# Weight conversion moved to VectorE alone, beside the first attention, staged through DRAM and read back by every batch, with longer key and query rows

## The chip, the cores and the metric

The kernel runs on one core of a Trainium2 chip. Its time is the device time of one execution in microseconds (us). Before the change it was 932.59 us as the median of 3 runs (931.72 to 932.88).

## The reference, cut to what matters

```python
# attention: batch 4, 8 heads, 768 tokens, head size 64; block-sparse
#   local scores (|i-j| < 16) and scores against 24 block maxima of k,
#   one softmax over both, times v and the block means of v
x = attention(q, k, v)                       # (4, 768, 512)
# Fourier mix and a channel MLP
u  = x + real(fft(fft(x, axis=1), axis=2))
un = (u - mean(u)) / sqrt(var(u) + 1e-6)
out = u + maximum(un @ w_ch1, 0) @ w_ch2     # w_ch1 512 x 2048, w_ch2 2048 x 512, both float64
```

The inputs q, k and v are float32. The two weight matrices come as float64 and have to be turned into float32 on the core, from pairs of 32-bit integers.

## The kernel before

Each batch goes through attention (four steps of two heads), a Fourier part, a layer norm, and a channel part. The channel part computes both products by the seven-product scheme for 2x2 blocks, so it needs sums of weight blocks: seven 128x256 pieces a block. There are 16 weight blocks: eight of the first matrix and eight of the second. The channel part is cut in four stages: `h` with half of the first matrix, `o` with half of the second, and again. TensorE does batch b's channel part while the attention of batch b+1 is interleaved. A scheduler orders the built instructions by itself.

Batch 0 has to make the weights. A block is two conversions (four VectorE steps, two ScalarE steps, one GpSimd multiplication each) and four GpSimd sums. They go straight into the buffer that batch 0 reads, and one write-back puts the block into DRAM for batches 1 to 3.

In the profile lines PE is TensorE, DVE VectorE, ACT ScalarE, POOL GpSimd and SPq SyncE's queue of transfers. `raw` are the integers as loaded, `cvt` the steps of a conversion, `w` a weight block in its buffer, `m` a staged block, `dw` its copy in DRAM, `s` sums of h for the second product, `kn` the keys as loaded, `km` their block maxima. `y` are Fourier products, `hx`, `hy`, `hz` products with the first matrix, `ox`, `oy`, `oz` with the second. The "fold" is VectorE's sums that open the Fourier part.

```python
def convert(name, dst, src, shape):                      # half a block: 128 x 512
    raw = bpool.tile([P, n, 2], I32, tag="raw", bufs=2)
    nc.sync.dma_start(out=raw..., in_=src)
    # 2 VectorE bit operations, 2 ScalarE activations, 2 VectorE operations (lines 687 to 693)
    gtt(dst, vb, va, ALU.mult)                           # GpSimd

def make_w1(j):
    w = bpool.tile([P, 7, 2, P], FP, tag="w1", bufs=3)   # the buffer batch 0 multiplies from
    for hh in range(2):
        convert(f"1_{j}_{hh}", w[:, 2 * hh:2 * hh + 2]..., src, (NDT, P))
    _left_sums(gtt, lambda i: w[:, i])                   # 4 sums on GpSimd
    nc.sync.dma_start(out=dw1[j], in_=w)                 # one write-back
    wt[1, 0, j] = w
# make_w2 likewise, tag "w2", 4 buffers

def load(b, g):                                          # rows of 64 floats = 256 bytes
    for dst, src in ((kn, k), (qn, q)):
        for e in range(2):
            nc.sync.dma_start(out=dst[:, :, e, :], in_=src[b, 2 * g + e].rearrange("(t p) d -> p t d", p=P))
...
    drive((gen_attention(0), 1))
    get_tables(0)                    # tables of the Fourier products
    drive((gen_weights(0, 3), 1))    # three blocks
    for b in range(B):
        gens = [(gen_post(b), 4)]    # Fourier part and channel part, four steps a round
        if b == 0:
            gens.append((gen_weights(3, None), 1))   # one block a round
        if b + 1 < B:
            gens.append((gen_attention(b + 1), 1))
        drive(*gens)
```

Of the kernel before, what the change touches and what calls it, by code (L numbers as in the profile page):

```python
# [469 lines left out]
def _main_program(ctx, tc, q, k, v, moe_w_ch1, moe_w_ch2, out):  # L470
# [63 lines left out]
    def load(b, g):  # L534
        qn, kn = (apool.tile([P, NST, 2, D], FP, tag="nat", bufs=4, name=f"{n}n_{b}_{g}") for n in "qk")
        for dst, src in ((kn, k), (qn, q)):
            for e in range(2):
                nc.sync.dma_start(out=dst[:, :, e, :], in_=src[b, 2 * g + e].rearrange("(t p) d -> p t d", p=P))
        nat[b, g] = qn, kn
# [42 lines left out]
    def prepare(b, g):  # L582
# [3 lines left out]
        for src, dst in ((kn, kt[:, W:W + S]), (qn, qt)):  # L586
            for h in range(2):
                ps = abank([P, HT, P], f"qk_{b}_{g}_{h}")
                for i in range(HT):
                    nc.tensor.transpose(ps[:, i, :], src[:, HT * h + i].rearrange("p e d -> p (e d)"), ident)  # L590
                nc.scalar.copy(out=dst[:, S2 * h:S2 * (h + 1)], in_=ps.rearrange("p i c -> p (i c)"))
# [33 lines left out]
    def values(b, g, p, pm, x):  # L625
# [19 lines left out]
        for r in range(2):  # L645
            rc = rec[:, b * NP + g, r]
            nc.vector.reciprocal(out=rc, in_=av[r][:, :, D])
            for h in range(2):
                ts, c = slice(HT * h, HT * (h + 1)), P * g + D * (r ^ h)
                tt(x[:, ts, c:c + D], av[r][:, ts, 0:D], rc[:, ts, None].to_broadcast([P, HT, D]), ALU.mult)  # L650
# [25 lines left out]
    wt = {}  # L676

    def convert(name, dst, src, shape):
# [17 lines left out]
        gtt(dst, vb, va, ALU.mult)  # L696

    def make_w1(j):

        w = bpool.tile([P, 7, 2, P], FP, tag="w1", bufs=3, name=f"w1_0_{j}")  # L700
        for hh in range(2):
            c = DF // 2 * hh + P * j
            src = moe_w_ch1.bitcast(I32)[:, 2 * c:2 * (c + P)].rearrange("(d p) n -> p d n", p=P)
            convert(f"1_{j}_{hh}", w[:, 2 * hh:2 * hh + 2].rearrange("p a d n -> p (a d) n"), src, (NDT, P))
        _left_sums(gtt, lambda i: w[:, i])
        nc.sync.dma_start(out=dw1[j], in_=w)
        wt[1, 0, j] = w

    def make_w2(j):

        w = bpool.tile([P, 7, HD], FP, tag="w2", bufs=NC, name=f"w2_0_{j}")
        for hh in range(2):
            r = P * (NJ * hh + j)
            convert(f"2_{j}_{hh}", w[:, 2 * hh:2 * hh + 2], moe_w_ch2.bitcast(I32)[r:r + P, :].rearrange(
                "p (a n) -> p a n", a=2), (2, HD))
        _right_sums(gtt, lambda i: w[:, i])
        nc.sync.dma_start(out=dw2[j], in_=w)
        wt[2, 0, j] = w

    def get_w1(b, j):  # L720
        w = bpool.tile([P, 7, 2, P], FP, tag="w1", bufs=3, name=f"w1_{b}_{j}")
        nc.sync.dma_start(out=w, in_=dw1[j])
        wt[1, b, j] = w

    def get_w2(b, j):
        w = bpool.tile([P, 7, HD], FP, tag="w2", bufs=NC, name=f"w2_{b}_{j}")
        nc.sync.dma_start(out=w, in_=dw2[j])
        wt[2, b, j] = w

    def gen_weights(first, last):  # L730

        steps = [(f, j) for c in range(0, NJ, NC) for f in (make_w1, make_w2) for j in range(c, c + NC)]
        for f, j in steps[first:last]:
            f(j)
            yield
# [4 lines left out]
    def get_tables(b):  # L740
        tag, bufs = ("w1", 3) if b else ("w2", NC)
        fs = []
        for par in range(2):
            t = bpool.tile([P, 2, HT, F2 + 1], FP, tag=tag, bufs=bufs, name=f"fs_{b}_{par}")
            nc.sync.dma_start(out=t, in_=dr["fs"].ap()[par])
            fs.append(t)
        fd = bpool.tile([P, 6, HD], FP, tag=tag, bufs=bufs, name=f"fd_{b}")
# [4 lines left out]
    def gen_fourier(b):  # L752
# [28 lines left out]
        for par in range(2):  # L781
            for g in range(4):
# [10 lines left out]
                nc.vector.tensor_copy(out=tr[:, g, par:S2:2], in_=ps[:, F2:0:-1])  # L793
# [4 lines left out]
        for half in range(2):  # L798
# [24 lines left out]
            for _ in range(4):  # L823
                tt(z, y, y, ALU.mult)
                tt(z, z, var, ALU.mult)
                nc.vector.tensor_scalar(out=z, in0=z, scalar1=-0.5, scalar2=1.5, op0=ALU.mult, op1=ADD)
                tt(y, y, z, ALU.mult)
            norms.append((stat, y))

        for t in range(NST):  # L830
            half, i = divmod(t, HT)
            stat, y = norms[half]
            nc.vector.tensor_scalar(out=un[:, t, :], in0=x[:, t, :], scalar1=stat[:, i, 0:1], scalar2=y[:, i:i + 1],
                                    op0=SUB, op1=ALU.mult)
# [3 lines left out]
            (nc.scalar.copy if t % 2 else nc.vector.tensor_copy)(  # L838
# [5 lines left out]
    def gen_channel(b):  # L844
        x, u = x_of[b], wt["u", b]
        for c in range(NJ // NC):
            js = range(NC * c, NC * (c + 1))
            if b:
                for j in js:
                    get_w2(b, j)  # L850
            h = bpool.tile([P, NC, 2, S], FP, tag="h", name=f"h_{b}_{c}")
            for j in js:
                if b:
                    for n in range(j if j == 0 else j + 2, min(j + 3, NJ)):
                        get_w1(b, n)
# [10 lines left out]
                def relu(t):  # L866
                    nc.vector.tensor_scalar(out=t, in0=t, scalar1=0.0, scalar2=None, op0=ALU.max)  # L867
# [5 lines left out]
                relu(c11)  # L873
# [4 lines left out]
                nc.scalar.copy(out=c22, in_=Z)  # L878
                yield
                product(X, S3, T3, False, False)  # L880
                tt(c22, X, c22, ADD)
                relu(c22)
                product(Z, S4, B22, False, True)
                tt(c12, Z, c12, ADD)
                relu(c12)
                yield
                product(X, A22, T4, False, True)
                nc.scalar.activation(out=c21, in_=X, func=AF.Relu)
                yield
# [72 lines left out]
    drive((gen_attention(0), 1))  # L962
# [62 lines left out]
```

## Time and profile before

| | before |
|---|---|
| span of the profiled run | 929.2 us |
| first Fourier product / first channel product of batch 0 | 80.4 / 137.2 us |
| end of batch 0's channel part | 350.6 us |
| the four channel stages | 53.5, 62.1, 52.4, 45.4 us |
| batches 1 to 3 | 578.6 us |

The prediction below shows the view by stretches that these come from. The first line is from the page's list of engines: busy us, share of the span, instructions.

```profile
PE 829.2 (89%) x6386; PEld 618.3 (67%) x6386; DVE 530.3 (57%) x1158; ACT 168.8 (18%) x349; POOL 147.4 (16%) x142
```

The second is what the one queue from which SyncE issues nearly all transfers waited for in the first 330 us: line, releaser, us in total, times, longest.

```profile
SPq L706 <- POOL w L529: 60.6, 8, 17.9
SPq L717 <- POOL w L529: 48.2, 8, 10.7
```

Lines 706 and 717 are the write-backs. They stand 109 us waiting for GpSimd's sums.

### The profile page before, as it was taken

How to read it: one execution, taken by the hardware profiler on the slowest of the kernel's cores; microseconds unless marked ns; L12 is line 12 of the kernel's file. 1: busy time of each engine (PE TensorE's matmuls, PEld its weight loads, DVE VectorE, ACT ScalarE, POOL GpSimd, SP SyncE). 2: the span in 40 equal slices, each digit the busy share in tenths (PEclk: the TensorE clock that was granted, in tenths of full speed). 3: DMA queues.
4: the chain of work that ended last, by engine and by line, in shares of the span. 5: the costliest groups of instructions: out<-in, count | busy, mean ns of one | idle time of the engine just before them, and what ended most of it. 6: DMA issues, size and time to landing. Idle time of an engine off the chain costs nothing.

```text
span 929.2 us, 15289 instructions
## 1 busy us (share of the span) xinstructions
PE 829.2 (89%) x6386; PEld 618.3 (67%) x6386; DVE 530.3 (57%) x1158; ACT 168.8 (18%) x349; POOL 147.4 (16%) x142
## 2 busy tenths in 40 slices
PE   4778748687886799999999999999999997999997
PEld 3656634466753588657875888668857875587586
DVE  1366986799368964935423937635327556352252
ACT  2222312432023102221112012220021011200200
POOL 2230625567056700020000000000000000000000
PEclk9777859989898999999999999999999998999999
DMA  9995791777926508826162147321051161213101
GB/s 187 178 189 164 236 178 62 219 228 218 163 76 244 199 35 287 151 97 147 35 206 78 57 150 232 86 80 41 27 197 60 46 261 54 105 41 153 45 24 48
DMA packets 127917, 122.76 MB, mean 132 GB/s; under 512 B 102912, under 2 KB 111328, under 8 KB 127840
## 3 DMA queue, kind: packets, MB, share of 16 engines
q1 hardware_dynamic: 127296, 121.14, 46.9%
q8 instruction: 52, 0.85, 0.4%
q10 hardware_dynamic: 544, 0.56, 0.2%
q14 instruction: 25, 0.20, 0.1%
HBM read 100.71 MB, written 20.97 MB: 131 GB/s over the span
## 4 chain that ended last, share of the span: by engine, by line
PE 68%; DVE 20%; DMA 4%; POOL 3%; issue 3%; SPq 2%; ACT 1%; DVEq 0%; ACTq 0%; POOLq 0%
PE ox L906 17%; PE hx L863 15%; PE oz L906 8%; PE hz L863 7%; PE oy L906 4%; PE hy L863 4%; PE y L786 3%; DMA raw<-in_moe_w_ch_dram 2%; DVE cvt L688 2%; POOL w L529 2%; DVE cvt L693 2%; PE sc L606 2%; DVE cvt L691 2%; DVE x L526 2%; DVE cvt L687 2%
## 5 line engine op out<-in xcount | busy, mean ns | idle before, releaser
L863 PE MATMUL hx<-u,w 128*128 128x384 f32 x512 | 189.2, 500 | 15.5 <-ACT h L876 6.0
L863 PEld LDWEIGHTS hx<-u,w 128*128 128x128 f32 x512 | 97.9, 195 | 85.8 <-ACT h L876 8.9
L906 PE MATMUL ox<-w,h 128*128 128x256 f32 x384 | 93.9, 393 | 8.4 <-DVE x L526 7.9
L863 PE MATMUL hz<-u,w 128*128 128x384 f32 x256 | 96.6, 498 | 4.7 <-ACT h L878 4.7
L906 PE MATMUL ox<-w,s 128*128 128x256 f32 x384 | 92.8, 384 | 4.0 <-DVE x L526 3.5
L906 PE MATMUL oz<-w,s 128*128 128x256 f32 x384 | 93.0, 384 | 2.6 <-DVE s L526 2.6
L906 PEld LDWEIGHTS ox<-w,h 128*128 128x128 f32 x384 | 75.4, 197 | 22.8 <-DVE x L526 9.1
L906 PEld LDWEIGHTS ox<-w,s 128*128 128x128 f32 x384 | 72.0, 191 | 16.3 <-DVE x L526 5.6
L526 DVE TENSOR_TENSOR x<-ox,x 128x256 f32<-128x256 f32 x96 | 40.4, 422 | 74.2 <-PE ox L906 74.2
L906 PEld LDWEIGHTS oz<-w,s 128*128 128x128 f32 x384 | 73.3, 192 | 13.1 <-DVE s L526 2.9
L863 PEld LDWEIGHTS hz<-u,w 128*128 128x128 f32 x256 | 49.8, 195 | 40.3 <-POOL vb L529 5.3
L529 POOL TENSOR_TENSOR w<-cvt 128x512 f32<-128x512 f32 x32 | 43.6, 1364 | 133.2 <-DVE cvt L693 72.5
L529 POOL TENSOR_TENSOR w<-w 128x256 f32<-128x256 f32 x64 | 56.2, 893 | 3.1
L526 DVE TENSOR_TENSOR h<-hy,h 128x384 f32<-128x384 f32 x32 | 17.8, 555 | 67.5 <-PE hy L863 67.5
L526 DVE TENSOR_TENSOR h<-hx,h 128x384 f32<-128x384 f32 x32 | 17.8, 555 | 56.1 <-PE hx L863 56.0
L863 PE MATMUL hy<-u,w 128*128 128x384 f32 x128 | 46.5, 486 | 0.0
L906 PE MATMUL oy<-w,h 128*128 128x256 f32 x192 | 46.0, 380 | 0.3 <-POOL w L529 0.3
L606 PEld LDWEIGHTS sc<-qt,kt 64*64 64x64 f32 x1536 | 33.7, 157 | 12.7 <-issue 8.6
L606 PE MATMUL sc<-qt,kt 64*64 64x32 f32 x1536 | 36.7, 239 | 6.0 <-issue 3.7
L906 PEld LDWEIGHTS oy<-w,h 128*128 128x128 f32 x192 | 36.5, 191 | 5.8 <-POOL w L529 0.7
L867 DVE TENSOR_SCALAR h<-h 128x384 f32<-128x384 f32 x96 | 38.7, 404 | 2.9
L526 DVE TENSOR_TENSOR s<-h 128x512 f32<-128x512 f32 x48 | 39.2, 816 | 0.2
(92 smaller groups left out, 1043.3 us busy)
## 6 DMA issues: line engine op xcount, KB each, us to landing
w<-dw SPq DMA_DIRECT2D x48, 896.0 KB, 5.6
raw<-in_moe_w_ch_dram SPq DMA_DIRECT2D x32, 512.0 KB, 5.1
dw<-w SPq DMA_DIRECT2D x16, 896.0 KB, 4.3
vw<-in_v_dram SPq DMA_DIRECT2D x62, 192.0 KB, 5.7
kn<-in_k_dram SPq DMA_DIRECT2D x32, 192.0 KB, 5.3
qn<-in_q_dram SPq DMA_DIRECT2D x32, 192.0 KB, 5.2
vb<-in_v_dram SPq DMA_DIRECT2D x16, 384.0 KB, 6.3
out_dram<-x SPq DMA_DIRECT2D x24, 256.0 KB, 2.0
```

Source lines behind the costliest of these rows:

```text
L526: nc.vector.tensor_tensor(out=out, in0=in0, in1=in1, op=op)
L529: nc.gpsimd.tensor_tensor(out=out, in0=in0, in1=in1, op=op)
L606: nc.tensor.matmul(ps[h][r:r + 64, i, :], kt[rows, o:o + 64], qt[rows, o:o + BLOCK], start=True, stop=True)
L687: nc.vector.tensor_scalar(out=ex, in0=high, scalar1=0x7FF00000, scalar2=None, op0=ALU.bitwise_and)
L688: nc.vector.tensor_scalar(out=man, in0=high, scalar1=0x000FFFFF, scalar2=None, op0=ALU.bitwise_and)
L691: nc.vector.scalar_tensor_tensor(out=ex, in0=high, scalar=-(1 << 31), in1=ex, op0=ALU.bitwise_and, op1=ALU.bitwise_or)
L693: nc.vector.scalar_tensor_tensor(out=tmp[:, 1, :], in0=low, scalar=2.0 ** -52, in1=tmp[:, 1, :], op0=ALU.mult, op1=ALU.add)
L786: nc.tensor.matmul(y, fgs[par][:, st, P * g:P * (g + 1)], fs[par][:, g % 2, st, :], start=(st == 0), stop=(st == HT - 1))
L863: nc.tensor.matmul(ps, w[:, a, kk, :], u[:, r, kk, :], start=start and kk == 0, stop=stop and kk == 1, skip_group_check=True)
L867: nc.vector.tensor_scalar(out=t, in0=t, scalar1=0.0, scalar2=None, op0=ALU.max)
L906: nc.tensor.matmul(ps, left[a][:, n, :], wt[2, b, j][:, r, :], start=start and n == 0, stop=stop and n == NC - 1, skip_group_check=True)
```

## The change

Its intent: take GpSimd off VectorE's shared ports by converting on VectorE alone; begin the conversion where VectorE is idle, beside the first attention; free the making of weights from the buffers that hold them, by staging each block in small buffers into DRAM and reading it back in batch 0 too; and load keys and queries in rows of 1536 bytes instead of 256. A few small operations move to ScalarE or become fewer.

```diff
-            nc.sync.dma_start(out=dst[:, :, e, :], in_=src[b, 2 * g + e].rearrange("(t p) d -> p t d", p=P))
+            nc.sync.dma_start(out=dst, in_=src[b, 2 * g:2 * g + 2].rearrange("e (p t) d -> p e (t d)", p=P))
 ... prepare(): 8 ScalarE copies of 64 x 384 instead of 4 of 128 x 384 a group
-        gtt(dst, vb, va, ALU.mult)
-    def make_w1(j): ...
-    def make_w2(j): ...
+        tt(dst, vb, va, ALU.mult)
+    def gen_weights():
+        for c, f, j in [...]:
+            t = [bpool.tile([P, 2, HD], FP, tag="s", bufs=5, ...) for i in range(2)]
+            for hh in range(2):
+                convert(..., t[hh]...)
+                if hh == 0:
+                    yield
+            t += [... two more "s" buffers]
+            (_left_sums if f == 1 else _right_sums)(tt, lambda i: t[i // 2][:, i % 2])
+            for i, n in enumerate((2, 2, 2, 1)):
+                nc.sync.dma_start(out=to[:, 2 * i:2 * i + n], in_=t[i])     # four write-backs
+            yield
 ... batch 0 calls get_w1 and get_w2 (read-back) as batches 1 to 3 do; its tables use the "w1" buffers
 ... Newton: 3 x 3 + 1 small instructions instead of 4 x 4; half of the scalings on ScalarE;
 ... h clamps of batch 0 and mirrored Fourier copies on ScalarE; two divisions by the row sums in one
-    drive((gen_attention(0), 1))
+    weights = gen_weights()
+    drive((gen_attention(0), 1), ((next(weights) for _ in range(12)), 1))   # six blocks
     get_tables(0)
-    drive((gen_weights(0, 3), 1))
...
-            gens.append((gen_weights(3, None), 1))
+            gens.append((weights, 2))                                        # two half blocks a round
```

## The prediction

> **What bounds the kernel now.** I read first the view that cuts the span at the first Fourier product of each batch (80.4, 350.6, 549 and 746 us) and, inside batch 0, at the first product with each half of the weights: us, then busy us (and instructions) of the engines, granted TensorE clock, DMA share, GB/s.
>
> ```profile
> core 0: us, PE busy (x) PEld busy (x) DVE busy (x) ACT busy (x) POOL busy (x), PEclk, DMA share, GB/s
> 0.00:60.00 60.00, 39.74 (x975) 32.45 (x976) 16.77 (x57) 15.39 (x33) 13.48 (x18) 0.86 1.04 184
> 60.00:80.40 20.40, 12.91 (x272) 9.33 (x271) 16.36 (x33) 4.15 (x9) 4.38 (x4) 0.56 1.08 251
> 80.40:137.20 56.80, 40.37 (x362) 33.99 (x359) 47.63 (x116) 17.35 (x34) 23.67 (x23) 0.71 0.72 176
> 137.20:190.70 53.50, 43.27 (x233) 25.47 (x232) 39.97 (x62) 19.16 (x36) 26.11 (x27) 0.93 0.50 149
> 190.70:252.80 62.10, 52.00 (x400) 41.56 (x399) 50.09 (x82) 13.73 (x24) 29.75 (x27) 0.89 0.80 198
> 252.80:305.20 52.40, 40.94 (x113) 22.85 (x112) 37.77 (x51) 15.92 (x29) 29.88 (x29) 0.90 0.48 153
> 305.20:350.60 45.40, 39.72 (x195) 33.06 (x194) 35.80 (x61) 1.73 (x3) 14.28 (x10) 0.96 0.36 121
> 350.60:549.00 198.40, 194.67 (x1571) 145.82 (x1570) 104.72 (x253) 31.55 (x71) 5.86 (x6) 1.00 0.45 127
> 549.00:746.00 197.00, 195.14 (x1595) 146.21 (x1594) 102.56 (x257) 30.02 (x68) 0.00 (x0) 1.00 0.33 106
> 746.00:929.00 183.00, 170.43 (x686) 127.56 (x684) 78.62 (x191) 19.77 (x43) 0.00 (x0) 0.97 0.24 92
> ```
>
> There are two kernels in this one. From 350.6 us on TensorE is busy 560 of 578 us at a clock near 1: only 18 us are open there. Batches 1 and 2 do one batch's channel work plus the next one's attention in 197 to 198 us. Before 350.6 us the same kind of work (one more attention, some 25 us) takes 350 us, so about 125 us are stall or half clock. A change to the preparation of weights can only be worth something there.
>
> Within it, two limits. Up to 80 us the DMA engines are full:
>
> ```profile
> DMA packets 42640, 16.14 MB, mean 202 GB/s; under 512 B 40291, under 2 KB 41539, under 8 KB 42627
> q1 hardware_dynamic: 42083, 15.39, 102.2%
> ```
>
> Nine tenths of the packets of these 80 us are short ones, the 256-byte rows of q, k and v. Averaging the packet records of the trace, a 256-byte packet took 26 ns of an engine there, a 1024-byte one 56 ns (later), a 2048-byte one 90 ns, a 4096-byte one 245 ns.
>
> From 80 to 350 us it is VectorE and GpSimd together. One line each for two VectorE steps of the conversion and for GpSimd's multiplications (minimum/median/maximum ns):
>
> ```profile
> L688 DVE TENSOR_SCALAR cvt<-raw x32: 413/946/1502, 86.2 to 312.2; 128x512 int32<-128x512 int32 x32
> L693 DVE SCALAR_TENSOR_TENSOR cvt<-raw,cvt x32: 677/679/2836, 87.8 to 313.7; 128x512 f32<-128x512 uint32 x32
> L529 POOL TENSOR_TENSOR w<-cvt x32: 1260/1296/1698, 88.5 to 314.5; 128x512 f32<-128x512 f32 x32
> ```
>
> The same instruction on the same shape takes 0.41 us or 1.5 us: VectorE is being held up, and in order of time the long ones coincide with a GpSimd instruction. The waits of TensorE in this stage end on VectorE (the bracket is idle time and releaser):
>
> ```profile
> 74.64 1.67 PE L643 MATMUL av<-vs,psum 64*128 64x130 f32 x12 [3.96 <-DVE vs L526]
> 234.77 5.44 PE L906 MATMUL ox<-w,h 128*128 128x256 f32 x12 [3.82 <-DVE x L526]
> 325.71 3.50 PE L906 MATMUL ox<-w,h 128*128 128x256 f32 x8 [3.78 <-DVE x L526]
> ```
>
> After such a wait twelve products take 5.44 us where twelve later ones take 2.6: the stall is paid again in clock.
>
> **What the Trainium skill says.** "SBUF — State Buffer", section "Who interferes with whom": VectorE instructions in a 2-port mode, or with two SBUF inputs, share a port pair with GpSimd, and one side blocks fully. The trace agrees (0.41 against 1.5 us above). "DMA: Bandwidth & Descriptors", section "Specifications", asks for at least 512 bytes per transfer for line rate; the trace agrees in direction: 256 B in 26 ns is 9.8 GB/s per engine, 4096 B in 245 ns is 16.7. "TensorE: Matmul & The Clock Gate", section "What's actually happening": an idle TensorE falls to half clock; the 5.44 us above and the 0.56 in the second row agree.
>
> **The change, part by part.**
> 1. *GpSimd leaves the conversion.* Removed: 32 multiplications and 64 sums on GpSimd (43.6 + 56.2 us by the groups of costs). Added on VectorE: 32 of 128x512, 0.68 us each as the undisturbed sums of that shape in batches 2 and 3 (21.8), and 64 of 128x256 at 0.42 us (26.9, the duration of the undisturbed x sums of that size). Gained: the four VectorE steps cost 110 us now; at their minima (0.41 + 0.41 + 0.67 + 0.68) they cost 69.5. Net +8 us. The `h` clamps of batch 0 go to ScalarE (24 x 0.54 = -13 us), the mirrored Fourier copies too (-3), and other VectorE work in the stage loses its contention (`s` sums 0.89 to 1.2 us against 0.68, folds 1.2 against 0.95: about -12). So VectorE's 244 us before 350 us become some 225 although it does everything alone. This is the gain, but spread, not on one wait.
> 2. *Six weights are issued beside the first attention.* By the order of the built instructions four of 16 weight blocks stand before the first fold on VectorE. One costs 2 x 2.85 + 4 x 0.42 = 7.4 us, in starts some 6.5; four are 26 to 30 us, on an engine busy 16.8 of the first 60 us. It fits, if the raw bytes come.
> 3. *Longer rows.* A group's q and k are 3072 packets of 256 B now (5.0 us of 16 engines), then 512 of 1536 B (73 ns each, interpolated: 2.3 us). For the five groups loaded before the fold that saves 13 us. But the four blocks ask for eight raw loads (8 x 512 packets x 56 ns / 16 = 14 us) and write-backs (2.6 us each, 8 to 10 us). A full DMA stage gets 10 us fuller, and the first fold, at 59.7 us now, comes at about 74.
> 4. *Order on the queue and on VectorE.* In the new order the tables for the Fourier products are issued behind the write-back of the first second-matrix block, and a whole such block (6.5 us) stands on VectorE between the fold and the value sums that release TensorE. Fold 11 us, block 6.5, sums and the score products: first Fourier product at 98 instead of 80.4.
> 5. *The Fourier part of batch 0*: the order puts six more blocks (40 us of VectorE) between its steps; I take 52 us against 56.8. Channel work starts at 150 against 137, but with 10 blocks done where before there were four (8 of the 32 steps of line 688 lie before 137 us).
> 6. *The four channel stages*: 53.5 + 62.1 + 52.4 + 45.4 = 213 us now. TensorE's own work at full clock is 36 us each plus attention pieces (8 + 12 in the first two). I estimate 50 + 59 (two blocks stand before the first `s` sums, a stall of about 9) + 38 + 38 = 185. Batch 0 ends at 335 instead of 350.6: -15 us.
> 7. *Read-back in batch 0*: 16 more loads of 896 KB, 14.7 MB; landing takes 5.6 us and the DMA share there is 0.4 to 0.8. Hidden.
> 8. *Batches 1 to 3.* Newton's steps for the square root go from 4 x 4 to 3 x 3 small instructions plus one; half of the scalings go to ScalarE. In batch 3 this chain runs from 767.3 to 774.5 us with TensorE half idle: about -4. Batches 1 and 2 have 2 to 4 us of idle each: -1.5 each. Doubled ScalarE copies for q and k (8 of half height instead of 4 per group, 2 us more) have room: ScalarE is busy 32 of 198 us.
> Sum: -15 - 7 = -22, 932.6 to about 910.
>
> **Rivals.**
> *VectorE becomes the bound of batch 0 from the start.* It now is in the path of attention, conversion and Fourier, in order. For it: the raw loads stand behind buffer waits on one queue, so VectorE can idle on a load while an attention step stands behind it. Against it: its total falls. If the Fourier products start only at 110 us, the time is 922 to 930.
> *The first attention does not slow.* If loads hide as they did, the fold starts at 63 us and everything shifts by 11: 898. Together with channel stages at 43 us each once the contention is gone, 886.
> *The transfers take over.* The write-backs share five small buffers with the `s` sums; a write lands in 4.3 us but 6 to 7 in the full stage. If each block waits for the one before, blocks come every 12 us and the stage gives nothing: 932.
>
> **Range and chances.** The end is the sum of two uncertain terms: start of the Fourier products (98, by 10 either way) and stalls after it (by 10 either way), added in squares 14 us; later batches add 3. I put 909, nudged one down as my walk took loads at their slow landing, with 888 to 928 as the range. 2% lies at 914: faster 0.6, same 0.37, slower 0.03.
>
> **What would show it.** Right: VectorE's conversion steps all near 0.41 and 0.68 us; first Fourier product between 90 and 106 us; ten blocks converted before the first channel product; third and fourth channel stage under 40 us each; the next batch's Fourier products at 325 to 345; batches 1 to 3 together at 570 to 574 us. Wrong if the first Fourier product stays near 80 us, if TensorE waits for `w` loads in the channel stages, or if batches 1 and 2 lengthen by waits on the doubled ScalarE copies.

## The result, and the profile after

The changed kernel gives the right result and takes 941.0 us (940.05 to 942.08, 4 runs) against 932.15 us (928.89 to 932.88, 4 runs) of the kernel before on the same chip. The ratio is 1.010, with a 95% interval of 1.0075 to 1.013. A ratio is the mean time of one kernel's fast runs over that of the other's of the same rounds, so it is not quite the ratio of the medians quoted. The kernel is 1% slower; I had said 909 and a range up to 928.

The stretches of batch 0 after, with the columns of the first fence of the prediction. I cut at the first fold (83.7 us), the first Fourier product, the first product of each channel stage, and the next batch's first Fourier product.

```profile
0.00:83.70 83.70, 55.95 (x1020) 43.59 (x1020) 46.73 (x106) 37.71 (x71) 16.11 (x20) 0.68 0.87 218
83.70:114.80 31.10, 12.60 (x230) 9.46 (x226) 25.65 (x53) 10.61 (x20) 2.10 (x2) 0.55 0.72 208
114.80:166.40 51.60, 39.28 (x358) 31.67 (x358) 43.71 (x108) 22.53 (x48) 5.37 (x5) 0.79 0.76 248
166.40:214.70 48.30, 43.69 (x337) 25.99 (x335) 33.90 (x72) 24.63 (x49) 0.00 (x0) 0.96 0.81 271
214.70:292.10 77.40, 56.88 (x486) 46.74 (x485) 47.23 (x94) 18.86 (x35) 10.49 (x9) 0.80 0.78 211
292.10:328.20 36.10, 36.10 (x113) 21.28 (x112) 7.12 (x13) 13.45 (x27) 5.41 (x6) 1.00 0.54 191
328.20:364.50 36.30, 36.30 (x170) 31.78 (x169) 25.81 (x54) 0.53 (x2) 0.00 (x0) 1.00 0.16 53
```

Read the first column down. The first Fourier product comes at 114.8 us instead of 80.4. The Fourier part itself is shorter (51.6 against 56.8), and so are the first, third and fourth channel stage (48.3, 36.1, 36.3 against 53.5, 52.4, 45.4). The second is longer: 77.4 against 62.1. Batch 0 ends 13.9 us later, and batches 1 to 3 are 4.9 us shorter (573.7 against 578.6). The gain is there where it was foreseen, and more than its size is lost in two places. Up to the first Fourier product TensorE has the same 1246 products as before; of the 34.4 us that they take longer, 18.5 are idle time, and 15.9 are products that take longer at a lower granted clock (busy 68.6 us at 0.65, before 52.7 us at 0.78).

One caution for all tables by stage: the attention of batch 1 is interleaved with batch 0, and the scheduler orders it anew in each kernel. The four channel stages hold 1106 products here and 941 before, of which the channel part itself has 560 in each. So some of the longer second stage, and of the shorter batches 1 to 3, is attention done earlier: in batches 1 to 3 TensorE is busy 556.4 us against 560.2. Only the whole time compares kernels cleanly.

What TensorE waited for in the first 115 us; in the first 80 us of the kernel before the wait for k was 7.1 us, and the tables were not waited for.

```profile
PE qk L591 <- DMA kn<-in_k_dram: 27.1, 4, 7.9
PE y L785 <- DMA fs<-c_fs: 3.9, 1, 3.9
```

The DMA engines are busy 0.87 and 0.72 in these rows, less than the 1.04 and 1.08 of before, so their mean load does not explain a late k. It was issued late. Here is SyncE's queue (start us, duration us, what is issued), and its longest wait in the first 330 us (us in total, times, longest), to set beside the two lines of before:

```profile
37.00 2.26 SPq L721 DMA_DIRECT2D dw<-m  x3
39.35 1.99 SPq L578 DMA_DIRECT2D vw<-in_v_dram  x3
41.40 2.32 SPq L686 DMA_DIRECT2D raw<-in_moe_w_ch_dram  x2
43.76 0.69 SPq L538 DMA_DIRECT2D kn<-in_k_dram  x1
```

```profile
SPq L721 <- DVE m L526: 102.9, 34, 15.5
```

The write-backs (line 721) wait for VectorE's sums; the next raw load and the next k follow them. TensorE's two large waits in the second channel stage are of the same look, one for a read-back and one for the next batch's k:

```profile
229.14 1.22 PE L911 MATMUL ox<-w,h 128*128 128x256 f32 x2 [10.35 <-DMA w<-dw]
237.33 1.51 PE L591 MATMUL qk<-ident,kn 128*128 128x128 f32 x6 [6.12 <-DMA kn<-in_k_dram]
```

This made a tidy first theory, called head of line below: one queue, a write-back at its head that waits, urgent loads behind. The experiments leave little of it.

VectorE's steps did become short, as foreseen. These are groups of batch 0: busy us and mean ns of one.

```profile
L694 DVE SCALAR_TENSOR_TENSOR cvt<-raw,cvt 128x512 int32<-128x512 int32 x32 | 22.0, 689 | 6.5 <-ACT cvt L692 6.4
L691 DVE TENSOR_SCALAR cvt<-raw 128x512 int32<-128x512 int32 x32 | 13.6, 425 | 0.0
```

### The profile page after: what moved, and what is told of

It reads as the page before. It is cut to its first block, busy times and chain, and to the rows that moved or that the text cites. A ratio compares the mean times of both kernels' runs of the same rounds, so it can differ in the third digit from the quotient of the medians.

```text
span 938.2 us, 15352 instructions
## 1 busy us (share of the span) xinstructions
PE 837.2 (89%) x6386; PEld 625.4 (67%) x6386; DVE 498.1 (53%) x1106; ACT 233.1 (25%) x481; POOL 46.8 (5%) x46
## 5 line engine op out<-in xcount | busy, mean ns | idle before, releaser
L865 PE MATMUL hx<-u,w 128*128 128x384 f32 x512 | 184.6, 491 | 1.8 <-DVE h L526 1.5
L911 PE MATMUL ox<-w,h 128*128 128x256 f32 x384 | 90.0, 381 | 10.3 <-DMA w<-dw 10.3
L865 PE MATMUL hz<-u,w 128*128 128x384 f32 x256 | 93.9, 487 | 1.3 <-DVE u L526 1.3
L526 DVE TENSOR_TENSOR x<-ox,x 128x256 f32<-128x256 f32 x96 | 40.6, 423 | 80.5 <-PE ox L911 80.4
L591 PE MATMUL qk<-ident,kn 128*128 128x128 f32 x96 | 18.6, 343 | 33.9 <-DMA kn<-in_k_dram 33.3
L608 PE MATMUL sc<-qt,kt 64*64 64x32 f32 x1536 | 40.9, 247 | 9.0 <-ACT p L612 4.9
L608 PEld LDWEIGHTS sc<-qt,kt 64*64 64x64 f32 x1536 | 38.1, 167 | 15.6 <-issue 8.9
L875 ACT COPY h<-hx 128x384 f32<-128x384 f32 x32 | 15.3, 479 | 124.9 <-PE hx L865 122.9
L591 PEld LDWEIGHTS qk<-ident,kn 128*128 128x128 f32 x96 | 13.9, 176 | 45.1 <-issue 42.9
L791 ACT COPY big<-y 128x192 f32<-128x192 f32 x32 | 10.7, 334 | 133.2 <-PE y L785 133.2
L692 ACT ACTIVATE cvt<-cvt,rebias 128x512 int32<-128x512 int32 x32 | 23.1, 720 | 72.9 <-DVE cvt L690 72.8
```

Of the source, the lines that this page charges most:

```text
L526: nc.vector.tensor_tensor(out=out, in0=in0, in1=in1, op=op)
L591: nc.tensor.transpose(ps[:, i::HT], src[:, e, P * i:P * (i + 1)], ident)
L608: nc.tensor.matmul(ps[h][r:r + 64, i, :], kt[rows, o:o + 64], qt[rows, o:o + BLOCK], start=True, stop=True)
L692: nc.scalar.activation(out=ex, in_=ex, func=AF.Relu, bias=rebias, scale=8.0)
L791: nc.scalar.copy(out=ty[:, g, par:S2:2], in_=y[:, 0:F2])
L865: nc.tensor.matmul(ps, w[:, a, kk, :], u[:, r, kk, :], start=start and kk == 0, stop=stop and kk == 1, skip_group_check=True)
```

## The experiments

Theories at the start: (1) head of line on SyncE's queue, as above; (2) VectorE works in its built order, and weight steps stand ahead of steps that TensorE waits for; (3) the volume of the transfers; (4) the long rows themselves. All 18 runs gave correct results, each timed in three rounds beside the kernel before (medians 930 to 932 us).

### First call: is it the queue?

Write-backs from GpSimd's queue:

```diff
-                nc.sync.dma_start(out=to[:, 2 * i:2 * i + n], in_=t[i])
+                nc.gpsimd.dma_start(out=to[:, 2 * i:2 * i + n], in_=t[i])
```

> The changed kernel, with one thing altered: the four write-backs of each weight block are issued from GpSimd's queue instead of SyncE's. Theory 1 (head of line): in the changed kernel a write-back waits on SyncE for VectorE's sums, and the k, q, v, table and raw loads that were issued behind it come late; then TensorE's 27 us of waits for k in the first 115 us shrink below 10 us, the first fold comes by 70 us instead of 83.7, the first Fourier product by 98 us instead of 114.8, and the time falls by 12 to 20 us, to 921 to 929. Theory 2 (VectorE, which runs in order, is what is late, with weight work standing ahead of attention's steps): the loads come earlier but nothing starts earlier; first Fourier product at 110 us or later, time 936 to 944. Theory 3 (the volume of the transfers): the same bytes, so the same 936 to 944.

Measured: 923.3 us, ratio 0.992 (0.989 to 0.995). The wait for k fell from 27.1 to 9.9 us, and the time is what theory 1 said. But the place is not: the first Fourier product came at 107.8 us, not below 98, and the first channel product at 166.6 us, no earlier than the 166.4 of the changed kernel. The first fold came at 79.4 us, not by 70. The gain lies in the channel stages (172 us together against 198, but with 919 products against 1106), and batches 1 to 3, with the attention left over, took 583.1 us against 573.7.

Long rows alone on the kernel before:

```diff
 (the kernel before, with load() and prepare() of the changed kernel)
```

> The kernel before, with the longer key and query rows alone. If the rows are worth what my prediction said (13 us of full DMA engines in the first 60 us), the first fold comes some 8 to 13 us before its 59.7 us and the time is 919 to 926. Theory 4 (the rows themselves cost: one load has to land whole before the first transpose, and ScalarE copies twice as many pieces): the first fold is not earlier than 59 us, and the time is 932 to 940.

Measured: 927.7 us, ratio 0.9965 (0.9935 to 0.9994). The time lies between the two ranges; the first fold, at 59.8 us, is not earlier, as theory 4 said. The first Fourier product comes at 78.7 us instead of 80.4: the rows saved 1.7 us there, not 13. In the first 60 us the trace has 11,500 packets fewer, and the engines' summed packet time did not fall (1000 us before, 1007 now, for 184 and 201 GB/s): the mean of the remaining 256-byte packets rose from 25.9 to 31.6 ns, and a 1536-byte packet took 88 ns, where I had interpolated 73 (in the changed kernel it took 75).

The changed kernel with short rows:

```diff
 (the changed kernel, with load() and prepare() of the kernel before)
```

> The changed kernel with the short rows of the kernel before. Theory 1: the queue is held up all the same and its transfers take longer: 941 to 955. Theory 3 (volume): the attention stage gets 13 us longer still, 950 to 958. Theory 4 (the long rows are what made the changed kernel slow): 925 to 935, with waits for k below 15 us in the first 115 us.

Measured: 949.8 us, ratio 1.021 (1.019 to 1.024), inside the range of theory 1 and just under that of theory 3. The first Fourier product comes at 122.4 us, 7.6 later. The long rows are not what made the changed kernel slow: in it they save 9 us.

The six blocks made after the first attention instead of beside it:

```diff
-    drive((gen_attention(0), 1), ((next(weights) for _ in range(12)), 1))
+    drive((gen_attention(0), 1))
     get_tables(0)
+    drive(((next(weights) for _ in range(12)), 1))
```

> The changed kernel with the first twelve weight steps (six blocks) issued after the first attention and the table loads, not beside the attention. Theories 1 and 2 (either the queue or VectorE makes the weight work beside attention dear): the first fold comes at 50 to 60 us, the first Fourier product at 72 to 85 us, and waits for k in that time stay below 10 us; the first channel product then waits for the first block and comes at about 135 to 150 us instead of 166; time 920 to 932. Theory 3 (volume): the bytes have to be moved all the same, so what is gained at the first Fourier product is given back by the first channel product: 936 to 944.

Measured: 945.5 us, ratio 1.017 (1.014 to 1.020). All three expectations of the time missed, theory 3's by little, though it put the loss before the first channel product, which came 14 us earlier (152.4). The first Fourier product came at 78.3 us, 36.5 us earlier, as theories 1 and 2 said. Then the Fourier part took 74.1 us instead of 51.6 and the first channel stage 62.4 instead of 48.3, and the second channel stage began at 214.8 us, where the changed kernel had begun it at 214.7. Thirty-six microseconds won in the first attention were worth nothing at the end, since the six blocks now stand in the Fourier part instead. Taking away the 27 us wait for k is not enough.

### Second call: which transfers, and staging at all

Only the key and query loads moved to GpSimd's queue:

```diff
-            nc.sync.dma_start(out=dst, in_=src[b, 2 * g:2 * g + 2]...)
+            nc.gpsimd.dma_start(out=dst, in_=src[b, 2 * g:2 * g + 2]...)
```

> The changed kernel with only the key and query loads moved to GpSimd's queue; the write-backs stay on SyncE, in front of the raw, value, table and read-back loads. If the late k loads of the first attention are what costs (27 us of TensorE waits before 115 us), the first Fourier product comes at 95 to 108 us and the end moves by as much: 922 to 934. If what is lost in the first attention is made up before the first output stage anyway (the first runs: the kernel with the write-backs moved began its first Fourier product 7 us earlier and its first channel product not at all), only the 6 us wait for k in the first output stage is won and the 10 us wait for the read-back stays: 932 to 938.

Measured: 955.4 us, ratio 1.026 (1.023 to 1.029), worse than either theory. The loads wait on GpSimd for a free buffer (181 us in 330), and GpSimd's own value sums stand behind them: TensorE waited 9.4 us for those sums, and the first Fourier product came at 135.2 us.

Only the read-backs moved:

```diff
-        nc.sync.dma_start(out=w, in_=dw1[j])      (and dw2)
+        nc.gpsimd.dma_start(out=w, in_=dw1[j])
```

> The changed kernel with only the read-backs of the converted weights moved to GpSimd's queue; the write-backs stay on SyncE. Expected if the 10.3 us wait for w in the first output stage comes from a read-back that stands behind a later block's write-back: everything up to 214 us as in the changed kernel, then that wait under 3 us and the stage near 67 us instead of 77; time 929 to 934. If the read-back itself (its bytes and its landing) is what is waited for, no change: 938 to 944.

Measured: 941.0 us, ratio 1.011 (1.007 to 1.015). The wait for w is gone from TensorE's waits, as expected, and nothing was gained: the second stage got to 55 us, but the two stages before it ran 56.4 and 57.0 us. Batch 0 ended 6 us earlier (358.3), and batches 1 to 3 took 9 us longer (582.9 us against 573.7), with 190 products more. A wait taken away in one place was paid in others.

Both edits, write-backs on GpSimd and six blocks after the attention:

```diff
 (the edits of the first and the fourth experiment)
```

> Both edits together: write-backs on GpSimd's queue, and the first six blocks made after the first attention. If the making of the weights as a whole sets the start of the first output stage (the two kernels with and without weight work beside attention both reached it at 214.8 us), the first Fourier product comes at about 78 us but the output stage at 205 to 215 us, and the time is that of the write-backs alone, 918 to 928. If the stall of the first attention is a cost of its own, the 30 us earlier start shows at the end: 898 to 912.

Measured: 940.8 us, ratio 1.011 (1.008 to 1.014). Both expectations missed. The Fourier part took 82.6 us here, with TensorE waiting 23.2 us at one place for the block maxima of k, which VectorE computes.

No staging. The blocks are made straight into their buffers in the order of the kernel before. The buffers of batch 0's tables and the order of the read-backs in batches 1 to 3 go back with that; everything else of the change is kept:

```diff
-    def gen_weights(): (staged)          get_w1 / get_w2 in batch 0
+    def make_w1(j) / make_w2(j): as before, with tt (VectorE) for gtt (GpSimd)
-    drive((gen_attention(0), 1), ((next(weights) for _ in range(12)), 1))
+    drive((gen_attention(0), 1))
     get_tables(0)
+    drive((gen_weights(0, 3), 1))
...
-            gens.append((weights, 2))
+            gens.append((gen_weights(3, None), 1))
```

> The changed kernel without staging: VectorE alone converts, longer rows, fewer Newton steps and the moves to ScalarE stay, but batch 0 makes its weights straight into the buffers it reads them from, in the order of the kernel before, and writes one copy of each block. If staging (with its queue order and read-back) is what ate the gain, the channel stages come near 40 us and the time is 905 to 920. If VectorE alone is simply too slow for the conversion, the channel stages stay above 50 us and the time is 928 to 945.

Measured: 892.2 us, ratio 0.9585 (0.956 to 0.961), beyond what I expected of it. Staging with its order, and with the two things that go back with it, costs 49 us, and the rest of the change gains 38. The stretches (same columns; first Fourier product at 77.4 us, then the Fourier part and the four channel stages):

```profile
77.40:129.60 52.20, 40.34 (x356) 33.79 (x353) 42.05 (x107) 23.57 (x49) 7.36 (x5) 0.75 0.68 182
129.60:176.90 47.30, 43.45 (x239) 24.89 (x238) 38.76 (x72) 24.61 (x48) 5.89 (x5) 0.93 0.70 210
176.90:236.70 59.80, 49.87 (x448) 40.33 (x447) 47.33 (x107) 18.21 (x33) 5.10 (x5) 0.94 0.74 208
236.70:271.90 35.20, 35.20 (x110) 20.31 (x109) 26.87 (x59) 19.39 (x38) 4.78 (x4) 1.00 0.60 210
271.90:314.80 42.90, 42.24 (x239) 35.19 (x238) 34.69 (x73) 7.75 (x15) 0.00 (x0) 1.00 0.27 99
```

This kernel has three blocks done before its first channel product and makes the other thirteen in the channel stages, and those take 185.2 us (1036 products). The changed kernel has nine done and takes 198.1 (1106 products). Work done early was not work saved: in the channel stages VectorE makes blocks while TensorE multiplies, and has room for it.

### Third call: the order, or staging itself

Staged, in the order of the kernel before (three blocks after the attention):

```diff
-    drive((gen_attention(0), 1), ((next(weights) for _ in range(12)), 1))
+    drive((gen_attention(0), 1))
     get_tables(0)
+    drive(((next(weights) for _ in range(6)), 1))
```

> The changed kernel, staged as it is, with the order of the kernel before: tables first, then three blocks (six steps) after the first attention, the rest between the later work. The kernel without staging, in this order, took 892. If the order (weight work made ahead of attention and Fourier steps on VectorE and in SyncE's queue) is what cost 49 us, this kernel takes 892 to 905, with the first Fourier product near 78 us and the first output stage near 180. If staging itself (small buffers, four write-backs a block, read-back) costs it, 920 to 945, and the first output stage begins after 200 us or has waits for w above 8 us.

Measured: 933.7 us, ratio 1.005 (0.999 to 1.011). Staging itself costs most of it: 41 of the 49 us. The first Fourier product comes at 79.2 us, but the Fourier part takes 75.2 us instead of 52.2. VectorE's instructions in it, in order of time (start us, duration):

```profile
120.93 0.69 DVE L526 TENSOR_TENSOR x<-mx,x 128x512 f32<-128x512 f32 x1
121.53 0.42 DVE L690 TENSOR_SCALAR cvt<-raw 128x512 int32<-128x512 int32 x1
121.86 0.42 DVE L691 TENSOR_SCALAR cvt<-raw 128x512 int32<-128x512 int32 x1
122.19 0.16 DVE L823 SCALAR_TENSOR_TENSOR norm<-norm 128x3 f32<-128x3 f32 x1
122.27 0.69 DVE L812 BATCH_NORM_STATS2 bst<-x 128x6 f32<-128x512 f32 x1
122.87 0.68 DVE L694 SCALAR_TENSOR_TENSOR cvt<-raw,cvt 128x512 int32<-128x512 int32 x1
123.46 0.69 DVE L696 SCALAR_TENSOR_TENSOR cvt<-raw,cvt 128x512 f32<-128x512 uint32 x1
124.06 0.16 DVE L526 TENSOR_TENSOR norm<-norm,stat 128x3 f32<-128x3 f32 x1
```

The layer norm's chain of 0.16 us steps (`norm`) advances by one step each time some 2 us of conversion (`cvt`) and of other large steps have gone by. The block maxima of k stand in the same line, and TensorE waits for them 14.7 us. The Trainium skill says why nothing overtakes: "PSUM — Partial Sum Buffer", section "Engine vs sequencer instructions", calls VectorE's queue strictly first in, first out. The trace agrees: the steps run back to back in the built order.

So why are there more weight steps there? In the kernel without staging the fourth block of the first matrix needs one of three `w1` buffers, and the first of them is released by the channel products. The buffers hold the weights back. In the kernel before, the trace shows it: GpSimd's multiplications into `w` stood idle 53.0 us for products of the first matrix, in two waits (busy us, mean ns, then idle us and what ended it).

```profile
L529 POOL TENSOR_TENSOR w<-cvt 128x512 f32<-128x512 f32 x32 | 43.6, 1364 | 133.2 <-DVE cvt L693 72.5 <-PE hx L863 53.0 <-DVE norm L821 3.2
```

Staged blocks need only small buffers, so nothing holds them back, and six blocks (9 in the changed kernel) stand on VectorE ahead of the first channel product, where the kernels that are held back have three.

The same with the write-backs on GpSimd's queue:

```diff
 (the edit above and that of the first experiment)
```

> As the run with the staged kernel in the order of before, and its write-backs issued from GpSimd's queue. If write-backs ahead of urgent loads in SyncE's queue are the cost of staging, it is 10 to 25 us faster than with them on SyncE. If what staging costs is the read-back or VectorE's order, the two agree within 5 us.

Measured: 933.3 us, ratio 1.003 (0.998 to 1.008), the same as without. This speaks against theory 1 in this order, but does not exclude it: on GpSimd's queue the write-backs waited 154 us for VectorE's sums, in front of GpSimd's own work, and that has a price of its own (below, 22 us). No run issued them from a third engine.

No staging, with the first three blocks beside the first attention:

```diff
-    drive((gen_attention(0), 1))
+    drive((gen_attention(0), 1), (gen_weights(0, 3), 1))
     get_tables(0)
-    drive((gen_weights(0, 3), 1))
```

> The kernel without staging (892 us), with its first three blocks made beside the first attention. If weight work beside attention is a cost by itself, the first Fourier product comes 10 to 25 us after its 77.4 us and the time is 900 to 915; if it fills open time of VectorE (busy 21 of the first 60 us), the first Fourier product stays below 85 us, the Fourier part shortens, and the time is 880 to 890.

Measured: 902.7 us, ratio 0.971 (0.966 to 0.977), 10.5 us slower than after the attention. The first Fourier product came at 103.4 us, 26 us later, and the first channel product at 137.6, 8 later. Here theory 1 has a large part: TensorE waited 4.4 us for k without these blocks, and with them in the first 110 us

```profile
PE qk L591 <- DMA kn<-in_k_dram: 18.6, 3, 11.2
```

For VectorE it waited less (3.2 us against 6.3). Of the 26 us, 10 are idle time of TensorE, and 16 are the same products at a lower granted clock (busy 70.8 us at 0.63, against 55.1 at 0.82).

No staging, with its 16 write-backs from GpSimd's queue:

```diff
-        nc.sync.dma_start(out=dw1[j], in_=w)      (and dw2)
+        nc.gpsimd.dma_start(out=dw1[j], in_=w)
```

> The kernel without staging (892 us), with its 16 write-backs issued from GpSimd's queue. If write-backs that wait for VectorE hold up the loads behind them on SyncE here too (30 us of SyncE's waits in the first 330), 882 to 889. If no urgent load stands behind them, 890 to 895.

Measured: 913.9 us, ratio 0.9815 (0.977 to 0.986): 21.7 us slower, against both expectations. GpSimd stood 175 us waiting to issue write-backs, in front of its own value sums. How that turns into each of the longer stages I did not trace.

### Fourth and fifth call: a brake, and the parts of the gain

A brake on the staged kernel. Three blocks after the attention, none further until the Fourier part has been issued, then three steps a round:

```diff
+    def gated(g):
+        while "go" not in wt:        # set between gen_fourier(b) and gen_channel(b)
+            yield
+        yield from g
-            gens.append((weights, 2))
+            gens.append((gated(weights), 3))
 ... each read-back as soon as its block has been written
```

> The staged kernel with a brake: three blocks after the first attention, and no further one until the Fourier part of batch 0 has been issued; then three steps a round instead of two, and each read-back as soon as its block has been written. If staging costs because nothing holds the weights back, so that six to nine blocks stand on VectorE ahead of Fourier steps (start of the channel products against blocks done before: 129.6 us with 3, 154.4 with 6, 152.4 with 7, 166.4 with 9), this one starts its channel products at 126 to 136 us and takes 893 to 910. If the transfers of staging are the cost, the channel products start in time but wait for w later, and the time is 920 to 940.

Measured: 916.7 us (911.2 to 919.9), ratio 0.986 (0.980 to 0.992), between the two ranges. The first channel product came at 128.1 us, as said: the brake works, with all transfers of staging left in, and with the two small edits that go with it gives 17 us against the same order without it. (The profiled run is the fastest of the four.) The rest stays: waits for the read-back and for the `s` sums behind it, in the span from 78 to 330 us.

```profile
PE ox L923 <- DMA w<-dw: 11.5, 4, 7.3
PE oz L923 <- DVE s L526: 10.6, 2, 8.5
```

The kernel before with conversion and sums on VectorE, and nothing else changed:

```diff
-        gtt(dst, vb, va, ALU.mult)   _left_sums(gtt, ...)   _right_sums(gtt, ...)
+        tt(dst, vb, va, ALU.mult)    _left_sums(tt, ...)    _right_sums(tt, ...)
```

> The kernel before, with the conversion and its sums on VectorE alone and nothing else changed. My prediction gave this the gain (VectorE's total falls as the port contention goes, and the four channel stages shrink from 213 to 185 us, of which the clamps on ScalarE are a part): 900 to 915. If the gain of the kernel without staging (892) comes from the small moves and the rows instead, 922 to 935.

Measured: 898.1 us, ratio 0.966 (0.961 to 0.971). Three words changed give 32 us; the time lies 2 us below the range. In the kernel before, all 25 steps of line 688 that took over 0.6 us overlap a GpSimd instruction, and one of the 7 shorter ones does; here the mean of that step is 440 ns instead of 952. VectorE's total in batch 0 fell from 244 to 233 us, although it does 48 us more. What is not separated: a block is also ready sooner, as its multiplication took 1.36 us on GpSimd and takes 0.73 on VectorE.

No staging, with two blocks ahead and the rest held back, two a round:

```diff
-    drive((gen_weights(0, 3), 1))
+    drive((gen_weights(0, 2), 1))
-            gens.append((gen_weights(3, None), 1))
+            gens.append((gated(gen_weights(2, None)), 2))
```

> The kernel without staging (892 us), with two blocks instead of three ahead of the Fourier part, and the rest, two a round, held back until the Fourier part has been issued. If each block ahead of the channel products costs 6 to 8 us there and is absorbed later beside TensorE's products, the channel products start at 118 to 124 us instead of 129.6 and the time is 884 to 890. If VectorE is the limit of the channel stages by now, what is won is given back there: 890 to 896.

Measured: 891.1 us, ratio 0.9587 (0.954 to 0.964), the same as without the edit. The first channel product came at 123.5 us, 6 us earlier as expected, and 2 us of that were given back in the channel stages (187.2 us against 185.2). What became of the other 4 is within the scatter of the runs (889 to 894 us here, 891 to 895 there). The end agrees with the second expectation.

No staging, with short rows:

```diff
 (the kernel without staging, with load() and prepare() of the kernel before)
```

> The kernel without staging (892 us), with the short key and query rows of before. The longer rows alone gave 3.4 us on the kernel before and 9 on the staged one. If they save what they saved there, 894 to 902.

Measured: 883.9 us (882.0 to 885.4), ratio 0.950 (0.945 to 0.955). The expected sign was wrong: the long rows cost 8.3 us here. The costs lie mostly in batches 1 to 3 (570.1 us against 578.1, with nearly the same number of products). ScalarE's copies of q and k in batch 2, long rows first, then short rows (busy us, mean ns); the copies of k look the same:

```profile
L593 ACT COPY qt<-qk 64x384 f32<-64x384 f32 x12 | 6.0, 504 | 0.2
```

```profile
L591 ACT COPY qt<-qk 128x384 f32<-128x384 f32 x6 | 2.8, 502 | 0.0
```

A copy of half the partitions takes the same 0.5 us. ScalarE is busy 41 of 199 us there, yet TensorE waited 2.1 us in that stretch for ScalarE's `big` copies (1.4 + 0.7) and none for them with short rows. Of the 3.3 us by which the stretch is longer (198.7 against 195.4), those are the part that the waits name; that the q and k copies stand before the `big` ones is argued, not shown.

The brake, with write-backs on GpSimd's queue:

```diff
 (the edits of the brake and of the first experiment)
```

> The staged kernel with the brake (916.7 us), with its write-backs issued from GpSimd's queue. What the brake left over lies in the first output stage (82.6 us, with 11.5 us of waits for the read-back of w and 10.6 us for s sums behind it). If the read-backs are late because they stand in SyncE's queue behind write-backs that wait for VectorE, those waits fall below 4 us and the time is 895 to 908. If they are late because the blocks themselves are made late, or if GpSimd's own value sums now stand behind the write-backs (as where the kernel without staging lost 21 us that way), 912 to 930.

Measured: 917.4 us (912.4 to 921.2), ratio 0.983 (0.978 to 0.988), the same as with the brake alone. The waits for w fell to 0.4 us, but the first and third channel stage are longer (54.4 and 60.0 us against 44.9 and 43.6). Taking the write-backs off SyncE's queue does not win what the brake left over; what GpSimd's queue costs in exchange is not known here.

No staging, short rows, two blocks ahead:

```diff
 (the edits of the two experiments before the last)
```

> No staging, short rows (883.9 us), and two blocks instead of three ahead of the Fourier part with the rest held back. If the two edits add up as on the kernel with long rows (1 us from holding back), 880 to 886; if the channel products start 6 us earlier and that stays, 876 to 880.

Measured: 883.1 us (881.0 to 887.7), ratio 0.948 (0.944 to 0.952). The first channel product came at 118.4 us, 13.6 earlier than with three blocks ahead, and batch 0 ended 7.4 us earlier (304.9 against 312.3). Batches 1 to 3 took 6.8 us longer (576.9 against 570.1), so the end is that of the short rows alone; what gives the time back there was not traced. Both are 5% faster than the kernel before and 6% faster than the changed one.

## Why the prediction was wrong

The runs make a ladder, each rung a run with one more part of the change (ratio to the kernel before):

| kernel | ratio | step, at 930 us |
|---|---|---|
| before | 1 | |
| + conversion on VectorE alone | 0.966 | -32 us |
| + small moves (Newton, ScalarE) | 0.950 | -15 |
| + long rows | 0.9585 | +8 |
| + staging, in the old order | 1.005 | +43 |
| + six blocks beside the first attention | 1.010 | +5 (the intervals overlap) |

The steps hold for this order of adding. The rows gain 3 us on the kernel before and 9 on the changed one, and cost 8 without staging.

And the position of the first channel product goes with the blocks made before it. In the kernels whose first Fourier product comes at 77 to 81 us:

| blocks done | first channel product, us | kernels |
|---|---|---|
| 2 | 118.4, 123.5 | no staging, two ahead |
| 3 | 128.1 to 137.2 | before, and with one part added; no staging with three ahead; the brake |
| 6 | 152.4, 154.4 | staged, six blocks after the attention; staged, old order |
| 7 | 160.0, 163.2 | the same two with write-backs on GpSimd |

(Blocks are counted when their sums are finished. The expectation for the brake has 152.4 with seven; by this count it is six.) From three blocks on, a block costs 7 to 9 us there; the cleanest pair, the staged kernel with the brake and without (128.1 and 154.4), gives 8.8. That is about its VectorE time (7.5 us: two times 2.9 us of conversion and four sums of 0.42).

**Step 1, GpSimd leaves, was right.** The four VectorE steps took 71.2 us in the changed kernel (22.0 + 22.0 + 13.6 + 13.6; I said 69.5), and VectorE's total in batch 0 was 230 us by the stretches (I said some 225). Alone it was worth more than I gave the whole of batch 0.

**Step 2, "It fits", failed.** I compared busy shares: VectorE was idle for 43 of the first 60 us, and 30 us of blocks should go in. Three blocks alone, with no staging, moved the first Fourier product by 26 us, the first channel product by 8 and the end by 10. VectorE did have the room: TensorE waited for it 3.2 us there. What failed is the overlap on the queue. The blocks' raw loads and write-backs waited for VectorE in front of k (27 us of SyncE's waits in the first 110), TensorE waited 18.6 us for k, and its slower clock added the rest. My condition "if the raw bytes come" asked whether the blocks get their bytes, not what their transfers hold up.

**Step 3, the rows, failed in size and then in sign.** 13 us became 1.7 before the first Fourier product. A DMA share near 1 (1.04, and 1.05 with 11,500 packets fewer) was taken for a sum of fixed packet times; fewer packets made the others longer. The first fold came at 83.7 us, not 74.

**Step 4 was mis-sized**: from the fold to the first Fourier product 31.1 us, not 24, which with step 3's 9.7 makes 114.8 us where I said 98. The wait for k that came before it is shown; the first and fourth experiments show that it was not decisive.

**Step 5** was right in length (51.6 us, I said 52) and nearly in blocks (nine done, I said ten; the four that I read for the kernel before are blocks begun; three were finished). That blocks done early pay back later was its silent assumption, and it is the one that failed most. With ten done I expected 185 us of channel stages. The kernel without staging has three done and takes 185.2.

**Step 6** was right in three stages and failed in the second: 77.4 us against 59, of which waits for w and k are 16.5. Without staging the same stage took 59.8.

**Step 7, "Hidden", failed.** A read-back was waited for 10.3 us. Moving the read-backs took that wait away and no time, so its price at the end stays unproven. That TensorE waits for `w` was one of my signs of being wrong, and it came true.

**Step 8** came out in sum (573.7 us, I said 570 to 574), in part by luck. Batch 3 is 4.1 us shorter, as said. Batch 2 is 3.2 us longer (198.8 against 195.6), where I said 1.5 shorter: "have room" failed, a halved copy costs ScalarE as much as a whole one, and TensorE waited 2.1 us for ScalarE's `big` steps, another of my signs. Without staging the rows made the later batches 8 us longer. Batch 1 is 4.0 us shorter, but with 164 fewer products, done earlier.

The sum of the misses: 16.8 at the first Fourier product, less 0.4 in the Fourier part, plus 13.1 in the channel stages make the 29.5 us by which batch 0 ended after my 335; later batches add 2.1.

Of the rivals, the first was nearest in its signs: VectorE in the path of all, first Fourier product after 110 us. It had 922 to 930 and no brake in it. The third named buffers that hold each other up; the runs show nearly the reverse: the lack of a holding buffer is the largest cost that a run isolates (17 us).

**What stays open.** Of the 43 us of staging, the brake shows 17. The other 25 or so come after it, with the channel stages at 213 and 206 us in the two braked kernels against 185 without staging (1244, 1028 and 1036 products, so part of the 213 is attention done early), and moving the write-backs to the other queue does not win them. Blocks that can be used only after a write (2.6 us to landing, median) and a read (6.1 us) are a candidate that no run tells apart from blocks made late. For the latter speaks that in 100 us around the braked kernel's second channel stage SyncE waited 55 us for VectorE in front of write-backs, and 8 us for writes to land in front of read-backs. Why the write-backs on GpSimd gave 18 us in the changed kernel and nothing in the staged kernel with the old order is not settled either: each edit also lets the scheduler order the rest anew.

## What to carry to other kernels

Before freeing work from a buffer that holds it back, ask what the buffer was doing: here three buffers kept non-urgent conversion out of the way of urgent steps on an engine that runs in order, and the conversion was hidden later anyway. Measure the parts of a bundled change one by one, since a gain of 5% stood beside a loss of 6% and the sum looked like nothing. A wait that the profile names is worth its length only if the next milestone moves when it is gone; look at the milestone, not at the wait, and at how much other work lies before it.

## What the Trainium skill lacked or had wrong

- "DMA: Bandwidth & Descriptors", section "Issuing engines are not separate DMA queues", says that issuing on several engines saves only the time of initiating a transfer. That section lacks that a transfer waiting for its data holds up whatever follows on its issuing engine. Moving transfers from SyncE to GpSimd changed the time by -18 us (write-backs, changed kernel), 0 (read-backs, changed kernel; write-backs, staged in the old order and with the brake), +14 (key and query loads) and +22 (write-backs, no staging).
- The same page, section "Specifications", asks for 512 bytes or more. It does not say what fewer packets are worth in a busy stage. Here those that stayed became longer: 256-byte packets took 25.9 ns on the mean in the first 60 us, and 31.6 ns once q and k came in 1536-byte ones; the first Fourier product gained 1.7 us.
- "ScalarE: Activation LUTs" has measured durations of an ACTIVATE for tiles of 128 partitions, but none for a copy of part of the partitions: 64x384 took 504 ns, 128x384 took 502 ns.
- None of the pages that I read says what work put ahead of urgent steps costs on an engine that works in order. The runs have the price: 7 to 9 us for each weight block of 7.5 us put ahead of the first channel product.
